# Scaling C's fifth and sixth tile, and one more scan's lam-multiples, on ScalarE in place of VectorE

## The chip, the core and the metric

The kernel runs on one core of a Trainium2 chip. A core has a matrix engine (TensorE, PE in the profile, with its weight loads as PEld), a vector engine (VectorE, DVE), a scalar engine (ScalarE, ACT), a general engine (GpSimd, POOL) and a queue engine (SyncE, SP). POOL and SP issue most of the DMA transfers here. Each engine takes its instructions in the order in which they are written; between engines, semaphores tell when a result, a buffer or a transfer is ready. The metric is the device time of one launch in microseconds (us), the median over runs.

## The reference

Two sequence models run on the same input x (2048 steps, 1024 channels, bf16), and a gate mixes them.

```python
x = A_x
g = sigmoid((x * gate_w).sum(-1, keepdims=True))

# a: a diagonal state space model with 1024 complex states
dt = exp(log_dt);  Lam_bar = exp(dt * Lam);  B_bar = ((Lam_bar - 1) / Lam)[:, None] * Bmat
Bu = einsum("bld,pd->blp", x, B_bar)
h_t = Lam_bar * h_{t-1} + Bu_t                      # for all 2048 steps
a = 2 * einsum("blp,dp->bld", h, Cmat).real + x * Dskip

# b: a short convolution of k (4 taps), times v, then a long convolution by FFT
kv = shift_conv(k, shift_k) * v
b = x * (irfft(rfft(kv) * rfft(ssm_k))[:2048] + kv * ssm_D)

out = g * a + (1 - g) * b
```

## The kernel before, in words

The first 200 us or so compute the long convolution b, by matrix products with tables of cosines, channel block by channel block, and store it in device memory (`cv_scr`). The change lies in what follows: the state space model.

**Tiles.** Time is cut into four blocks of 512 steps, each split into even and odd steps (256 each). The 1024 states are cut into four groups (g = 0 to 3) of two tiles of 128 states. C is therefore eight tiles, `CT[0]` to `CT[7]`, each with a real and an imaginary half of 128 x 1024; group g of the states uses tiles 2g and 2g + 1. B's factor and the factor 2 are folded into C: `turn_C(pi)` (line 1274) multiplies tile pi by a complex number per state. It writes the cross terms (C times `mc2i`) to two buffers `m` on ScalarE, scales C's halves in place by `c2r` and `mc2r`, and adds the two, for tiles 0, 1, 4 and 5 by a DMA that accumulates (`gather`, line 126, issued by POOL; the traces show it as `CT<-Q`), for the others by an addition on VectorE. For tiles 4 and 5, "C's fifth and sixth tile", the `m` buffers come from the pool `Q` of four buffers (line 1337); the traces name them `Q`.

**A Bu unit.** For one time block and one state tile, 16 matrix products fill a bank group of the accumulators (`both`, four such groups rotate), and ScalarE evicts it in two parts to the even steps V and the odd steps O of a tile U. `Bu_next` (line 1365) issues two units per pair of time block and group, and after each unit up to two "fillers": pieces of work taken from the list `on_act` (line 1443).

**A turn.** `turn_U` (line 872) adds lam times the odd steps before to the even steps, so that a scan over even steps alone suffices. It does so in two parts; each writes a buffer of the pool `Q` on ScalarE and adds it to V by a DMA (`U<-Q`). The second part's DMA writes what the first one wrote, and so waits for its landing.

**A scan.** `scan(tb, g, fin)` (line 891) is all VectorE: two products with cosines and sines, two sums, four scan instructions (`W`), and the way back to `hb`, the states at even steps. The states at odd steps are lam times `hb` plus O: four multiplies by lam into two buffers q (`scaled`, line 947), and three additions into O (`summed`, line 956). The list `scaled_by_act` (line 889) names the scans whose multiplies ScalarE does: scan 4 (counted over time block and group, 16 in all) and scans 12, 13 and 14. For these, `scaled` is called later from the main loop, and `summed` in the next scan, behind its four scan instructions (line 922). The buffers q come from VectorE's work pool, but for scans 12 to 14 from the pool `Q`.

**C times the states.** The product with C runs over rows of 128 steps in `psy`: the first two rows of a time block read `hb`, the last two read the odd steps. For the first time block it goes row by row (units C0 to C3), for the second and third group by group (units G10 to G23, where G23 is the third block's group 3), and the last block is done at the end. ScalarE evicts each row of a block times the gate (`scale_a`), and only then can its accumulator banks be used again. The row's part of b is loaded (`loads`: `pbb`, `xr`), scaled on ScalarE (`scale_b`), multiplied by x on VectorE (`product`) and added by a DMA.

**The order.** It is written out by hand. A loop over the 16 scans (j) advances scan j, runs the two tiles of C that are due, issues a turn, and then the units of `plan[j]` (line 1383): j = 1 has the Bu units B9 and B10, j = 2 has B11, j = 3 has B12, B13 and C0; j = 11 has G20, j = 12 has G21 to G23. The turns are set by `turned` (line 1385): turn 14 belongs to j = 10, turn 15 to j = 11. A pool gives its buffers in turn, in the order in which the program's instructions first use them, and an instruction that is to write a buffer waits until its last reader, here often a DMA, is through.

Of the kernel before, what the change touches and what calls it, by code (L numbers as in the profile page):

```python
# [20 lines left out]
def kernel(  # L21
# [39 lines left out]
    NTB = S // TB  # L61
# [30 lines left out]
    def put(eng, f, *a, **kw):  # L92
        with tc.issue_after(prev[eng]) if eng in prev else nullcontext():
            i = f(*a, **kw)  # L94
        prev[eng] = getattr(i, "ins", i)
# [4 lines left out]
    def bc(ap, shape):  # L100
        return ap.to_broadcast(shape)
# [3 lines left out]
    def tt(o, a, b, op):  # L105
        put("dve", V.tensor_tensor, out=o, in0=a, in1=b, op=op)
# [7 lines left out]
    def copy(o, a):  # L114
        put("dve", V.tensor_copy, o, a)

    def act(o, i, **kw):
        put("act", nc.scalar.activation, out=o, in_=i, **kw)
# [7 lines left out]
    def gather(o, i):  # L126
        put("pool", nc.gpsimd.dma_start, out=o, in_=i, accum_op=ALU.add)
# [628 lines left out]
    def carry(tb):  # L756
        q1 = consts.tile([128, 2, NP], F32, name="q1", tag="q1")
        q2 = consts.tile([128, 2, NP], F32, name="q2", tag="q2")
        w = WL[tb - 1]
        tt(q1, w, bc(cs["cU"][:, None, :], [128, 2, NP]), ALU.mult)  # L760
        tt(q2, w, bc(cs["sU"][:, None, :], [128, 2, NP]), ALU.mult)
        tt(init[tb][:, 0], q1[:, 0], q2[:, 1], ALU.subtract)
        tt(init[tb][:, 1], q1[:, 1], q2[:, 0], ALU.add)
# [122 lines left out]
            yield  # L886

    put_off = []
    scaled_by_act = (4, 12, 13, 14)

    def scan(tb, g, fin):


        last = tb == NTB - 1 and g == NG - 1
        Ve, Uo = Us[tb, g]
        A = w2([128, 2, 2, HB], BF16, "A")
        W = None

        for js in ([slice(0, 1), slice(1, 2)] if last else [slice(0, 2)]):
            g2 = slice(2 * g + js.start, 2 * g + js.stop)  # L900
            full = [128, 2, js.stop - js.start, HB]
            Aj, Uj = A[:, :, js], Ve[:, :, js]
            tt(Aj, bc(TC[:, g2][:, None], full), Uj, ALU.mult)
            if js.start == 0:
                yield
            b = w2([128, 2, 2, HB], BF16, "trn")[:, :, js]
            tt(b, bc(TS[:, g2][:, None], full), Uj, ALU.mult)
            if js.start == 0:
                if g == 0 and tb > 0:
                    carry(tb)  # L910
                step(fin)
            tt(Aj[:, 0], Aj[:, 0], b[:, 1], ALU.add)
            tt(Aj[:, 1], Aj[:, 1], b[:, 0], ALU.subtract)
            if W is None:
                W = w2([128, 2, 2, HB], BF16, "W")
            for j in range(js.start, js.stop):
                pi = 2 * g + j
                for c in range(2):
                    put("dve", V.tensor_tensor_scan, out=W[:, c, j], data0=bc(rv2[:, pi:pi + 1], [128, HB]),
                        data1=A[:, c, j], initial=0.0 if tb == 0 else init[tb][:, c, pi:pi + 1],  # L920
                        op0=ALU.mult, op1=ALU.add)
            while put_off:
                put_off.pop()[1]()
            if js.start == 0:
                run(fin)
                hbs[tb, g] = s5p["hb"].tile([128, 2, 2, HB], BF16, name="hb")
            hb = hbs[tb, g][:, :, js]
            Wj = W[:, :, js]
            tt(hb, bc(TC[:, g2][:, None], full), Wj, ALU.mult)
            if tb < NTB - 1:  # L930
                copy(WL[tb][:, :, g2], Wj[:, :, :, HB - 1])
            b = w2([128, 2, 2, HB], BF16, "trn")[:, :, js]
            tt(b, bc(TS[:, g2][:, None], full), Wj, ALU.mult)
            if not last:
                yield
            tt(hb[:, 0], hb[:, 0], b[:, 1], ALU.subtract)
            tt(hb[:, 1], hb[:, 1], b[:, 0], ALU.add)
            by_act = tb * NG + g in scaled_by_act
            if tb * NG + g == 3:
                run(turning[7])  # L940
                product(0)
            if by_act and tb == NTB - 1:
                q = [s5p["Q"].tile([128, 2, 2, HB], BF16, name="Q") for k in range(2)]
            else:
                q = [w2([128, 2, 2, HB], BF16, "q") for k in range(2)]

            def scaled(q=q):
                for k in range(2):
                    for j in range(js.start, js.stop):
                        a = (q[k][:, :, j], hbs[tb, g][:, :, j], lam[:, k, 2 * g + j:2 * g + j + 1])  # L950
                        if by_act:
                            act(a[0], a[1], func=ACT.Identity, scale=a[2])
                        else:
                            ts(*a, None, ALU.mult)

            def summed(q=q, js=js):
                o, (q1, q2) = Uo[:, :, js], [x[:, :, js] for x in q]
                tt(o, o, q1, ALU.add)
                tt(o[:, 0], o[:, 0], q2[:, 1], ALU.subtract)
                tt(o[:, 1], o[:, 1], q2[:, 0], ALU.add)  # L960

            if by_act:
                put_off.append((scaled, summed))
            else:
                scaled()
                summed()
# [66 lines left out]
    def product(t_):  # L1033
        pbb, xr = ios[t_]
        tt(xr, xr, pbb, ALU.mult)
# [4 lines left out]
    def store(t_):  # L1040
        move(rows_of(of, t_), gas.pop(t_))
# [23 lines left out]
    def step(gen):  # L1065
        next(gen, None)

    def run(gen):
        for _ in gen:
            pass  # L1070
# [203 lines left out]
    def turn_C(pi):  # L1274
        by_sum = pi in (0, 1, 4, 5)
        if pi in (4, 5):
            m = [s5p["Q"].tile([128, D], BF16, name="Q") for c in range(2)]
        else:
            whole_m = m_pool.tile([128, 2, D], BF16, name="m")
            m = [whole_m[:, c] for c in range(2)]  # L1280
        for c in range(2):
            act(m[c], CT[pi][:, 1 - c], func=ACT.Identity, scale=mc2i[:, pi:pi + 1])
            yield
        for c, f in enumerate((c2r, mc2r)):
            if pi < 2:
                act(CT[pi][:, c], CT[pi][:, c], func=ACT.Identity, scale=f[:, pi:pi + 1])
            else:
                ts(CT[pi][:, c], CT[pi][:, c], f[:, pi:pi + 1], None, ALU.mult)
            if by_sum:
                gather(CT[pi][:, c], m[c])  # L1290
        if not by_sum:
            tt(CT[pi], CT[pi], whole_m, ALU.add)

    turning = [turn_C(pi) for pi in range(NP)]
    load_BT(3, 0)
    load_BT(3, 1)
# [45 lines left out]
    def w2(shape, dt, name):  # L1342
        return wk.tile(shape, dt, name=name, tag="w2")
# [11 lines left out]
    on_act = []  # L1355
# [77 lines left out]
    for j in range(NS):  # L1433
        for k in loaded.get(j, ()):
            loads(k)
        if j == 7:
            store(3)
        for k in stored.get(j, ()):
            store(k)
        advance(j)  # L1440
        for t in turning[2 * j:2 * j + 2]:
            run(t)
        on_act += [lambda t=t: step(t) for t in turning[2 * j + 2:2 * j + 4] for _ in range(2)]
        turn = turns_U[turned[j]] if j in turned else none
        if j != 10 and plan[j][0:1] != "G":
            step(turn)
        by_group = plan[j][0:1] == "G" and j != 10
        if j == 7:
            scale_b(6)
        if by_group:  # L1450
            for n, k in enumerate(scaled_b.get(j, ())):
                if n == 1:
                    step(turn)
                scale_b(k)
            run(turn)
        if j == 4:
            put_off[-1][0]()
            scale_b(3)
        for unit in plan[j].split():
            if unit == "C0":  # L1460
                scale_b(2)
            if unit[0] == "G":
                Cy_group(int(unit[1]), int(unit[2]))
            else:
                (Bu_next if unit[0] == "B" else Cy_row)(int(unit[1:]))
        if put_off and j not in (4, 12):
            put_off[-1][0]()
        if j == 10:
            step(turn)
            for k in scaled_b[j]:  # L1470
                scale_b(k)
            run(turn)
        elif not by_group:
            run(turn)
            if j == 5:
                run(turns_U[5])
            for k in scaled_b.get(j, ()):
                scale_b(k)
        if j == 7:
            gate(3)  # L1480

    tb = NTB - 1
# [46 lines left out]
```

## Time and profile before

| | |
|---|---|
| median of 3 runs | 384.33 us (384.24 to 385.03) |
| the profiled execution, its own time | 384.57 us |
| its span, first to last instruction | 382.8 us |
| TensorE busy | 371.3 us (97%) |
| VectorE busy | 371.2 us (97%) |
| ScalarE busy | 303.6 us (79%) |
| GpSimd busy | 81.8 us (21%) |

The page gives busy times, the span in 40 slices, the chain of work that ended last, and groups of instructions. In a line such as `CT<-CT,c2r 128x1024 bf16` the tile written stands before the arrow, those read behind it. All operations go through a few helpers on one line of the kernel (L94), so groups are told apart by their tiles. Times in a timeline are counted from the span's start; a row "x4" merges four instructions, its length running from the first start to the last end, and consecutive instructions of VectorE and ScalarE overlap a little, so that the step from one start to the next is shorter than one instruction's length. A bracket at the end of a row gives the idle time of the engine before it and what ended that.

Where things stand in the timeline: the Bu units of j = 1 to 3 run on TensorE from 217.4 to 252, C0 begins at 253.2, G22 at 337.0, G23 at 343.9, the last time block at 350.8, and the last matrix product ends at 378.6.

### The profile page before, as it was taken

How to read it: one execution, taken by the hardware profiler on the slowest of the kernel's cores; microseconds unless marked ns; L12 is line 12 of the kernel's file. 1: busy time of each engine (PE TensorE's matmuls, PEld its weight loads, DVE VectorE, ACT ScalarE, POOL GpSimd, SP SyncE). 2: the span in 40 equal slices, each digit the busy share in tenths (PEclk: the TensorE clock that was granted, in tenths of full speed). 3: DMA queues.
4: the chain of work that ended last, by engine and by line, in shares of the span. 5: the costliest groups of instructions: out<-in, count | busy, mean ns of one | idle time of the engine just before them, and what ended most of it. 6: DMA issues, size and time to landing. Idle time of an engine off the chain costs nothing.

```text
span 382.8 us, 6633 instructions
## 1 busy us (share of the span) xinstructions
PE 371.3 (97%) x2419; PEld 198.3 (52%) x2453; DVE 371.2 (97%) x599; ACT 303.6 (79%) x469; POOL 81.8 (21%) x108
## 2 busy tenths in 40 slices
PE   7899999999999999999999999989999999999995
PEld 5566458575584846744454444434444444444442
DVE  7999999999999999999999999999999999999996
ACT  5898998988979999786979699675989759937601
POOL 4011030020301102031003110413414323634100
PEclk9999999999999999999999999999999999999999
DMA  7979999998999997959999999986899999898903
GB/s 166 165 108 223 218 205 205 245 203 211 201 164 211 208 213 169 198 125 154 192 221 164 226 203 250 213 153 125 150 222 192 208 245 246 136 250 156 238 8 110
DMA packets 126402, 71.77 MB, mean 187 GB/s; under 512 B 104665, under 2 KB 107489, under 8 KB 126370
## 3 DMA queue, kind: packets, MB, share of 16 engines
q1 hardware_dynamic: 111232, 45.64, 55.4%
q0 software_dynamic: 12976, 25.17, 38.9%
q10 hardware_dynamic: 2162, 0.54, 0.8%
q8 instruction: 19, 0.31, 0.3%
q14 instruction: 13, 0.11, 0.1%
HBM read 15.48 MB, written 8.39 MB: 62 GB/s over the span
## 4 chain that ended last, share of the span: by engine, by line
PE 52%; DVE 30%; issue 9%; DMA 4%; ACT 3%; ACTq 1%; POOL 0%; DVEq 0%; POOLq 0%
PE psy L94 29%; PE both L94 15%; DVE BT L94 11%; DVE wkh L94 8%; DVE G L94 5%; DVE t L94 3%; PE psz L94 2%; DVE ks L94 2%; PE psk L94 2%; DMA CT<-Q 2%; DMA pbb<-cv_scr 1%; PE psv L94 1%; DMA rows<-in_gate_w_dram 1%; PE p L94 1%; PE taps L94 1%
## 5 line engine op out<-in xcount | busy, mean ns | idle before, releaser
L94 PEld LDWEIGHTS <-BT 128*128 128x128 bf16 x640 | 62.0, 98 | 48.3 <-issue 0.2
L94 PE MATMUL both<-xT,BT 128*128 128x512 bf16 x375 | 83.0, 379 | 0.4
L94 POOL DMA_DIRECT2D U<-Q x26 | 26.7, 1039 | 88.8 <-ACT Q L94 31.0
L94 PEld LDWEIGHTS <-hb 128*128 128x128 bf16 x256 | 24.9, 98 | 31.4 <-issue 1.6
L94 PEld LDWEIGHTS <-U 128*128 128x128 bf16 x240 | 23.5, 98 | 28.3
L94 PE MATMUL psy<-CT,hb 128*128 128x512 bf16 x157 | 36.3, 379 | 0.1
L94 ACT ACTIVATE Vh<-psv 128x1024 bf16<-128x1024 f32 x32 | 30.7, 1034 | 5.3 <-PE psv L94 5.3
L94 PE MATMUL psy<-CT,U 128*128 128x512 bf16 x149 | 34.6, 379 | 0.2
L94 ACT ACTIVATE Q<-U,lam 128x512 bf16<-128x512 bf16 (+1 forms) x52 | 29.9, 612 | 4.9 <-DMA CT<-Q 4.9
L94 DVE TENSOR_TENSOR_SCAN W<-rv,init,A 128x256 bf16<-128x256 f32 x48 | 32.2, 730 | 0.0
L94 POOL DMA_DIRECT2D G<-wkh x8 | 9.7, 1218 | 102.8 <-DVE wkh L94 102.8
L94 ACT ACTIVATE U<-both 128x512 bf16<-128x512 f32 x44 | 24.1, 595 | 8.0 <-PE both L94 7.5
L94 PEld LDWEIGHTS <-SF 128*128 128x128 bf16 x184 | 18.0, 98 | 19.7 <-issue 1.4
L94 PE MATMUL psk<-eok,SF 128*128 128x512 bf16 (+1 forms) x119 | 27.9, 354 | 0.3
L94 PE MATMUL psz<-G,CI 128*128 128x512 bf16 x64 | 24.3, 379 | 0.1
L94 PE MATMUL psz<-G,SI 128*128 128x512 bf16 x64 | 24.3, 379 | 0.0
L94 PE MATMUL psy<-CTa,hb 128*128 128x512 bf16 x94 | 22.6, 379 | 1.2 <-ACT U L94 1.0
L94 PE MATMUL taps<-dg,kT 128*128 128x128 bf16 (+1 forms) x352 | 21.7, 210 | 0.8 <-DMA kT<-in_B_k_dram 0.8
L94 PEld LDWEIGHTS <-kT 128*128 128x128 bf16 x352 | 21.0, 100 | 2.5 <-DMA kT<-in_B_k_dram 2.1
L94 DVE TENSOR_TENSOR wkh<-BT,Vh 128x3072 bf16<-128x3072 bf16 (+4 forms) x20 | 21.8, 1110 | 0.0
L94 DVE TENSOR_TENSOR wkh<-Kh,Vh 128x3072 bf16<-128x3072 bf16 (+2 forms) x16 | 21.2, 1348 | 0.0
L94 PE MATMUL psy<-CTa,U 128*128 128x512 bf16 x87 | 20.4, 379 | 0.1
(227 smaller groups left out, 846.1 us busy)
## 6 DMA issues: line engine op xcount, KB each, us to landing
U<-Q POOLq DMA_DIRECT2D x26, 256.0 KB, 5.3
G<-wkh POOLq DMA_DIRECT2D x6, 768.0 KB, 8.8
cv_scr<-cv SPq DMA_DIRECT2D x16, 256.0 KB, 5.7
kn<-in_B_ssm_k_dram SPq DMA_DIRECT2D x5, 512.0 KB, 4.0
v<-in_B_v_dram SPq DMA_DIRECT2D x5, 512.0 KB, 6.2
out_dram<-m SPq DMA_DIRECT2D x8, 256.0 KB, 4.5
BT<-cv_scr SPq DMA_DIRECT2D x7, 256.0 KB, 5.9
out_dram<-BT SPq DMA_DIRECT2D x7, 256.0 KB, 2.0
```

What stands on the lines that cost most here:

```text
L94: i = f(*a, **kw)
```

## The change

Three edits belong together. First, `scaled_by_act` gets scan 11, the third time block's group 3: its four multiplies by lam are done by ScalarE, called at the end of the loop's pass j = 11, and its three additions move into scan 12. Its buffers q now come from the pool `Q` (the condition `tb > 1` in place of the last time block alone). Second, in `turn_C` the scaling by `c2r` and `mc2r` goes to ScalarE for tiles 0, 1, 4 and 5 (it was there already for 0 and 1), and a `yield` behind each half's `gather` cuts this work into pieces that can be fillers. Third, the fillers: tiles 4 and 5 are listed at j = 1 with four pieces each in place of two, so that scaling and additions go out between the Bu units of j = 1 and 2; at j = 0 nothing is listed any more (there tiles 2 and 3 were listed, whose pieces had run by the time the first filler was called).

```diff
-    scaled_by_act = (4, 12, 13, 14)
+    scaled_by_act = (4, 11, 12, 13, 14)
...
-            if by_act and tb == NTB - 1:
+            if by_act and tb > 1:
                 q = [s5p["Q"].tile([128, 2, 2, HB], BF16, name="Q") for k in range(2)]
             else:
                 q = [w2([128, 2, 2, HB], BF16, "q") for k in range(2)]
...
         for c, f in enumerate((c2r, mc2r)):
-            if pi < 2:
+            if by_sum:
                 act(CT[pi][:, c], CT[pi][:, c], func=ACT.Identity, scale=f[:, pi:pi + 1])
             else:
                 ts(CT[pi][:, c], CT[pi][:, c], f[:, pi:pi + 1], None, ALU.mult)
             if by_sum:
                 gather(CT[pi][:, c], m[c])
+                yield
...
-        on_act += [lambda t=t: step(t) for t in turning[2 * j + 2:2 * j + 4] for _ in range(2)]
+        if j > 0:
+            on_act += [lambda t=t: step(t) for t in turning[2 * j + 2:2 * j + 4] for _ in range(4 if j == 1 else 2)]
```

## The prediction

> **What bounds the kernel now.** I read the page first (shares of engines), then busy time by stretches, the waits, the chain of work that ended last, and then the timelines of single engines where the change lies.
>
> ```profile
> PE 371.3 (97%) x2419; PEld 198.3 (52%) x2453; DVE 371.2 (97%) x599; ACT 303.6 (79%) x469; POOL 81.8 (21%) x108
> 240.00:248.00 8.00, 8.00 (x39) 3.63 (x37) 7.89 (x20) 5.59 (x8) 3.26 (x5) 1.00 0.92 213
> 248.00:256.00 8.00, 6.91 (x33) 3.07 (x32) 7.93 (x16) 5.43 (x13) 2.11 (x3) 1.00 1.10 205
> 336.00:344.00 8.00, 7.95 (x38) 3.63 (x37) 7.93 (x19) 2.44 (x3) 3.46 (x4) 1.00 1.05 260
> ```
>
> The three lower lines are stretches: length, then busy time of TensorE, its weight loads, VectorE, ScalarE and POOL, the granted clock, the DMA share and GB/s. TensorE and VectorE are both full: 7.8 to 8 of 8 us in every stretch, but for TensorE at 248 to 256. ScalarE has room. Two full engines mean that work taken from one gains nothing by itself, and that any stall of either is felt.
>
> ```profile
> ACT Q L94 <- DMA CT<-Q: 4.9, 1, 4.9
> PE psy L94 <- ACT U L94: 1.0, 1, 1.0
> ...
> 244.74 5.78 DMA CT<-Q
> ...
> 251.17 0.71 ACT Q L94
> ...
> 253.15 9.01 PE psy L94 x41
> ...
> 374.96 3.63 PE psy L94 x16
> 378.62 0.75 DVE BT L94
> ```
>
> The first two lines are waits (us, times, longest), the rest the chain by start and length. At 244.74 the additions into C's fifth and sixth tile go out (they waited for VectorE's scaling), land at 250.5, ScalarE waits 4.9 us for the buffers that they read, evicts late, and TensorE starts `psy` late. From 253.15 to 378.6 TensorE runs without a gap and sets the end.
>
> ```profile
> 329.88 2.52 POOL L94 DMA_DIRECT2D U<-Q  x1
> 340.54 0.86 POOL L94 DMA_DIRECT2D U<-Q  x1 [7.25 <-DMA U<-Q]
> U<-Q POOLq DMA_DIRECT2D x1, 256.0 KB, 10.1
> U<-Q POOLq DMA_DIRECT2D x1, 256.0 KB, 6.0
> 345.63 2.56 ACT L94 ACTIVATE Q<-hb,lam 128x512 bf16<-128x512 bf16 x4 [7.19 <-DVE hb L94]
> 334.41 1.14 DVE L94 TENSOR_SCALAR q<-hb,lam 128x512 bf16<-128x512 bf16 x4
> 335.47 1.48 DVE L94 TENSOR_TENSOR U<-U,q 128x1024 bf16<-128x1024 bf16 x3
> 342.40 0.66 DVE L94 TENSOR_TENSOR row<-row 128x1024 bf16<-128x1024 bf16 x1
> 347.34 3.62 PE L94 MATMUL psy<-CT,U 128*128 128x512 bf16 x16
> 378.62 1.41 DVE L94 SCALAR_TENSOR_TENSOR BT<-psy,gcols,xlast 128x512 bf16<-128x512 f32 x2 [0.42 <-PE psy L94]
> ```
>
> The third and fourth line give the time from issue to landing of the two gathers above them, so turn 14's gathers land at 339.98 and 346.54. The ScalarE line is scan 12's multiples; the VectorE lines are scan 11's multiples and sum, and the first operation behind scan 12's scans. The last line: VectorE idles only 0.42 us before its last work.
>
> **Part 1, C's fifth and sixth tile.** (That j = 0 lists no fillers any more removes calls that did nothing: tiles 2 and 3 were through before the first filler ran.) VectorE loses four multiplies, 243.96 to 245.55: 1.59 us. ScalarE gets four of the kind of `m<-CT`, two of which take 2.08 from start to the next start: 4.16. They now stand between the evictions of the four `both` units of j = 1 and 2, each tile's pair behind the second of its units. ScalarE was busy from 225.51 to 245.53 with 0.14 idle; with 4.16 more, less that 0.14, it is through at 249.5. The first loads it needs earlier are there: the imaginary half of the fifth tile is issued at 220.51 and lands after 5.9, at 226.4; it is wanted at 226.7 (before: 229.16). The gathers go out between 231 and 239, land well before 249, and the wait of 4.9 us is gone: `Q<-U` starts at 249.4, not 250.54. TensorE follows its eviction as before: 253.15 - 1.12 = 252.03. Its units run from 217.41, 160 matmuls at 0.2157, to 251.9, so 0.1 of the wait stays. No earlier unit is starved: the tightest, the ninth, starts at 245.0 and needs an eviction that ends near 242.1. On POOL the four gathers pass `pbb<-gd`, which leaves at 241 in place of 237.3; VectorE multiplies that row at 255.9, so nothing waits. On the DMA engines the four gathers (1.3 us each, by the spacing of their landings) now fall among SP's loads of 231 to 243, whose share is already 1.07 there. The tightest of those, row 1's `pbb`, is issued at 235.9, lands after some 6.7 (its median) and with 4 us more at 246.6, and ScalarE wants it at 247.4. If it is later still, TensorE loses up to 1.1 again; the end does not depend on that, as part 2 shows. Part 1 alone: TensorE 1.1 us earlier, VectorE 1.6.
>
> The swap is dear by itself: a multiply of 128x1024 steps on by 0.40 us on VectorE and by 1.04 on ScalarE. [...]
>
> **Part 2, scan 11's multiples.** VectorE loses four multiplies (334.41 to 335.47, 1.06). Its sum (three additions, 1.39) moves behind scan 12's four scans. ScalarE gets four multiplies, 2.47 (the row of scan 12, start to next start), in its queue behind turn 15 and ahead of row 14's scaling, scan 12's multiples and the evictions of the third time block.
>
> What decides is where the multiples are written. They no longer go to the work pool but to the `Q` pool, four buffers. The changed program's instructions show which they get: those of turn 14, and the first pair waits for the landing of turn 14's first gather, the second pair for its second. In the old kernel scan 12 had these two buffers and found the second free at 346.54, just before it wrote it (346.87). Scan 11 wants it some 9 us earlier. So:
>
> - VectorE reaches the sum at 342.40 - 1.59 - 1.06 - 1.39 = 338.4.
> - The gathers move with their cause. Each second gather of a turn waits for the first one's landing, and so back to ScalarE at 266.68, which waits for scan 4's `hb` on VectorE, 1.6 earlier. I take the shift as 1.6: landings at 338.4 and 344.9.
> - ScalarE writes the first pair at 338.4 to 339.8 (VectorE waits 1.4), the second at 344.9 to 346.3 (VectorE waits 5.9, with one addition between). The last two additions take 0.7: VectorE does `row<-row` at 347.0 in place of 342.40, 4.6 late.
> - All that VectorE has left is in the old order and without a gap, so it ends 4.6 late less the 0.42 it idled: **4.2 us later**.
> - TensorE: the `U` that it wanted at 347.34 - 1.1 = 346.2 comes at 346.8. Then scan 12's `hb` ends at 345.54 + 4.6 = 350.2, its multiples on ScalarE 350.2 to 352.7, and only behind these come the evictions, the first done at 353.8. The last block's first matmul needs that bank: 353.9 in place of 350.79, 3.1 late; the second half of scan 15's `hb` adds 0.4. 3.5 is under 4.2: VectorE sets the end.
>
> **Sum.** Against the profiled execution (384.57, span 382.8): 384.57 + 4.2 = 388.8. It stands 0.24 above the median of the runs, 384.33; the forecast is 388.5.
>
> **Bounds.** Unknown are the shift and the landing time of turn 14's second gather. Shift 0: VectorE 6.2 late, end +5.8, 390.1. The shortest landing of any gather from `Q` is 3.3 (the tile's view: 3.3/5.4/10.1): issued at 338.9 it lands at 342.2, VectorE 1.9 late, +1.5, 385.8. I take 6.0, the row of this very gather, since the queue ahead of it is unchanged.
>
> **The rivals.**
> - Faster: the buffers are free in time and TensorE keeps its 1.1 us: 383.2. For it: VectorE is given 2.65 us and ScalarE idles from 338.4 to 345.6. It decides at a second landing of 340.7; the gather would have to land 1.8 us after its issue at 338.9, where none from `Q` took under 3.3. 0.07.
> - No change within measurement: a landing near 340.7 to 341.5. 0.03.
> - The gathers do not move with VectorE: 390.1. For it, the DMA queues are full at 304 to 320 and could hold the pace. Against it, the loads there wait on the same gathers. 0.13.
> - The gathers are quicker once the rest has thinned out: 385.8 to 387. 0.12.
> - TensorE's clock falls. After the last matmul (378.6) the granted clock is 1.00 until 380.8 and 0.50 from 381.0. The new gap before the last block, 350.3 to 353.9, is longer than those 2.4 us. [...] 0.25.
>
> **How the numbers follow.** The forecast itself 0.40, the others as given. 0.2% is 0.77 us, about what a measurement of this kernel can tell from no change: slower by more 0.90, within 0.03, faster 0.07. The range, from the shortest landing to no shift: 385.8 to 390.3.
>
> **What would show it.** ScalarE's `Q<-hb` of scan 11 in two halves near 338.4 and 344.9, with waits of about 3.3 and 5.3 us ended by the DMA `U<-Q`; VectorE waiting some 6 us in one piece at `U<-U,Q` for ScalarE; TensorE with a gap of about 3.5 us before the last block, and none of 1.0 at 252; the last chain on VectorE. The forecast is wrong if turn 14's second gather lands before 341, or if VectorE shows no wait over 1 us.

## The result and the profile after

| | before | after |
|---|---|---|
| median of the runs | 384.73 us (6 runs) | 388.75 us (6 runs) |
| ratio, 95% interval | | 1.0108 [1.0085, 1.0131] |
| the profiled execution, its own time | 384.57 us | 388.58 us |
| its span | 382.8 us | 386.8 us |

The changed kernel is 1.1% slower. The profiled executions differ by 4.01 us, and the last operation of VectorE ends 3.97 us later (384.00 against 380.03), so nearly all of it lies ahead of that operation. Here and below medians are over all runs, while ratios leave out the slow ones, those over 1.5% above the fastest of the same kernel, which is why a high median can stand beside a ratio of 1.

The engines' busy times, from the page of the changed kernel (busy time, share of the span, instructions):

```profile
PE 372.8 (96%) x2419; PEld 198.2 (51%) x2453; DVE 368.8 (95%) x591; ACT 310.5 (80%) x477; POOL 81.6 (21%) x108
```

VectorE lost 2.4 us of work and ScalarE got 6.9 more. TensorE has the same 2419 instructions; the 1.5 us by which it is busy longer are a stretch at a slower clock, shown below. The change did what its diff says; the time came from waiting and from that stretch. Stretches of the changed kernel show where (columns as in the prediction: busy time of TensorE, weight loads, VectorE, ScalarE, POOL, then the granted clock, the DMA share and GB/s):

```profile
240.00:248.00 8.00, 8.00 (x39) 3.64 (x38) 7.89 (x18) 7.94 (x13) 1.09 (x2) 1.00 1.12 235
248.00:256.00 8.00, 7.95 (x38) 3.56 (x38) 7.93 (x17) 7.97 (x15) 1.71 (x2) 1.00 0.80 175
336.00:344.00 8.00, 7.95 (x38) 3.63 (x38) 3.43 (x6) 1.33 (x2) 3.51 (x4) 1.00 1.09 251
344.00:352.00 8.00, 6.13 (x29) 2.67 (x28) 6.30 (x13) 5.83 (x8) 1.74 (x2) 1.00 0.73 129
352.00:360.00 8.00, 6.75 (x24) 2.79 (x25) 7.86 (x16) 6.70 (x10) 3.42 (x4) 0.79 0.69 133
```

At 240 to 256, where part 1 lies, ScalarE is now full and TensorE too: 7.95 of 8 us in place of 6.91. At 336 to 344 VectorE is busy for 3.43 us (before: 7.93) and ScalarE for 1.33: both wait. TensorE loses its time after that, first by standing still, then, in the last stretch, at a lower clock.

The waits of the changed kernel (us, times, longest) from the answers for ScalarE, VectorE and TensorE:

```profile
ACT Q L94 <- DMA U<-Q: 7.4, 2, 5.9
...
DVE U L94 <- ACT Q L94: 6.2, 1, 6.2
...
PE psy L94 <- ACT BT L94: 3.1, 1, 3.1
```

The two waits shown of before, `ACT Q <- DMA CT<-Q` and `PE psy <- ACT U`, are gone, and these three have come. They are one story, as the timelines of ScalarE, VectorE and TensorE tell:

```profile
337.06 1.33 ACT L94 ACTIVATE Q<-hb,lam 128x512 bf16<-128x512 bf16 x2 [1.52 <-DMA U<-Q]
344.30 1.33 ACT L94 ACTIVATE Q<-hb,lam 128x512 bf16<-128x512 bf16 x2 [5.90 <-DMA U<-Q]
349.59 2.56 ACT L94 ACTIVATE Q<-hb,lam 128x512 bf16<-128x512 bf16 x4 [1.88 <-DVE hb L94]
...
338.76 0.67 DVE L94 TENSOR_TENSOR U<-U,Q 128x1024 bf16<-128x1024 bf16 x1
345.67 0.76 DVE L94 TENSOR_TENSOR U<-U,Q 128x512 bf16<-128x512 bf16 x2 [6.24 <-ACT Q L94]
346.34 0.68 DVE L94 TENSOR_TENSOR row<-row 128x1024 bf16<-128x1024 bf16 x1
...
346.52 3.62 PE L94 MATMUL psy<-CT,U 128*128 128x512 bf16 x16
353.19 5.18 PE L94 MATMUL psy<-CTa,hb 128*128 128x512 bf16 x15 [3.06 <-ACT BT L94]
...
382.59 1.41 DVE L94 SCALAR_TENSOR_TENSOR BT<-psy,gcols,xlast 128x512 bf16<-128x512 f32 x2 [0.42 <-PE psy L94]
```

Scan 11's first pair of multiples waits until turn 14's first gather is through, the second pair until its second gather is. VectorE has done one of the three additions by then and stands for 6.24 us; `row<-row` starts at 346.34 in place of 342.40, 3.94 late. Scan 12 is late by that, its multiples stand on ScalarE ahead of the third block's evictions, and TensorE stands for 3.06 us in front of the last block. VectorE's last operation again waits 0.42 us for TensorE, so TensorE sets the end. The chain of work that ended last (start, length, what) runs back through all of it, to the two gathers:

```profile
327.41 9.55 DMA U<-Q
...
337.51 6.70 DMA U<-Q
...
344.30 1.34 ACT Q L94 x2
...
346.43 0.60 DVE row L94
...
352.14 1.01 ACT BT L94
...
353.19 4.10 PE psy L94 x11
...
378.93 3.63 PE psy L94 x16
```

### The profile page after: what moved, and what is told of

Same layout as the page of the kernel before. It is cut to its first block, busy times and chain, and to the rows that moved or that the text cites. A ratio compares the mean times of both kernels' runs of the same rounds, so it can differ in the third digit from the quotient of the medians.

```text
span 386.8 us, 6631 instructions
## 1 busy us (share of the span) xinstructions
PE 372.8 (96%) x2419; PEld 198.2 (51%) x2453; DVE 368.8 (95%) x591; ACT 310.5 (80%) x477; POOL 81.6 (21%) x108
## 4 chain that ended last, share of the span: by engine, by line
PE 42%; DVE 31%; DMA 10%; issue 8%; ACT 6%; POOL 1%; ACTq 1%; DVEq 0%; POOLq 0%
PE both L94 20%; PE psy L94 15%; DVE BT L94 11%; DVE wkh L94 8%; DMA U<-Q 7%; DVE G L94 5%; DVE t L94 2%; PE psz L94 2%; DMA V<-Q 2%; DVE ks L94 2%; PE psk L94 2%; ACT Q L94 2%; DMA rows<-in_gate_w_dram 1%; PE psv L94 1%; PE taps L94 1%
## 5 line engine op out<-in xcount | busy, mean ns | idle before, releaser
L94 PE MATMUL psy<-CTa,hb 128*128 128x512 bf16 x94 | 24.1, 399 | 3.2 <-ACT BT L94 3.1
L94 ACT ACTIVATE Q<-hb,lam 128x512 bf16<-128x512 bf16 x16 | 10.3, 711 | 13.7 <-DMA U<-Q 7.4
```

## The experiments

Each ratio is against runs of the kernel before on the same chip.

| kernel | median, us | ratio [95%] |
|---|---|---|
| part 1 alone | 384.49 | 0.9990 [0.9962, 1.0018] |
| part 1's places, VectorE scales | 384.30 | 0.9977 [0.9943, 1.0012] |
| part 2 alone | 389.56 | 1.0128 [1.0103, 1.0152] |
| part 2 alone, work pool | 385.57 | 1.0012 [0.9985, 1.0038] |
| the change, work pool | 386.78 | 0.9998 [0.9959, 1.0037] |
| the same, again | 385.17 | 0.9996 [0.9974, 1.0017] |
| the change, only the second pair in the work pool | 385.19 | 0.9997 [0.9971, 1.0023] |
| the change, TensorE's gap filled | 388.82 | 1.0099 [1.0069, 1.0129] |
| before, one spare buffer | 383.89 | 0.9968 [0.9939, 0.9996] |
| the same, again | 383.70 | 0.9964 [0.9944, 0.9985] |

### Part 1 alone

```diff
 # the changed kernel, with two of its lines as before
-    scaled_by_act = (4, 11, 12, 13, 14)
+    scaled_by_act = (4, 12, 13, 14)
...
-            if by_act and tb > 1:
+            if by_act and tb == NTB - 1:
```

> Part 1 alone: C's fifth and sixth tile as in the changed kernel, scan 11 as before. If the whole loss is scan 11's wait for turn 14's buffers: no wait of ScalarE for the DMA CT<-Q, TensorE's gap of 1.0 at C0 gone, 1.1 us faster than before (ratio 0.997). If moving the multiplies to the slower engine costs by itself: as slow as before or slower (1.000 to 1.005). If the earlier additions hold up other transfers: ScalarE late at j = 3, and the gap at C0 as before (1.000).

No change that can be measured; the interval, 0.9962 to 1.0018, still holds the 0.997 that was expected. In its trace VectorE is well ahead: `row<-row` starts at 340.31, 2.09 earlier than before. It gets nothing for it, as the last pieces of the chain show:

```profile
196.35 6.29 DMA BT<-in_A_B_im_dram
202.68 12.26 PE both L94 x56
214.94 3.45 PE psz L94 x16
218.40 34.53 PE both L94 x160
252.93 27.69 PE psy L94 x128
280.62 13.81 PE both L94 x64
295.22 83.07 PE psy L94 x384
```

TensorE runs from 202.68 to the end without a wait. C0 does not wait for ScalarE any more. This execution ends only 0.30 us earlier on TensorE than before's, since TensorE waited 1.18 us for a load of B at 202, which before's profiled execution did not. What that wait hides can be read by counting from the first `psz` matmul behind it: C0 starts 39.19 us after it in before's execution (253.15 less 213.96), 38.06 us after it here (252.84 less 214.78) and as much in the changed kernel (252.33 less 214.27). So TensorE does get the 1.1 us that were forecast for part 1.

### Part 1's places, with VectorE scaling

```diff
 # against part 1 alone
-            if by_sum:
+            if pi < 2:
                 act(CT[pi][:, c], CT[pi][:, c], func=ACT.Identity, scale=f[:, pi:pi + 1])
```

> Part 1's place without its engine: the fifth and sixth tile are scaled between the Bu units of j = 1 and 2 as in the changed kernel, but by VectorE; scan 11 as before. If it is the early release of the Q buffers that pays: the same as part 1 alone, 1.1 us faster than before (0.997), ScalarE through earlier by 4. If it is VectorE's 1.6 us: no faster than before (1.000).

Again no change that can be measured: the interval, 0.9943 to 1.0012, holds both values that were expected, 0.997 and 1.000. ScalarE's row for the turn, from the timeline, has no wait and starts 4.0 us earlier than before's (250.54); TensorE starts C0 behind the Bu units without one:

```profile
246.54 1.32 ACT L94 ACTIVATE Q<-U,lam 128x512 bf16<-128x512 bf16 x2
...
248.69 4.26 PE L94 MATMUL both<-xT,BT 128*128 128x512 bf16 x19
252.79 2.75 PE L94 MATMUL psy<-CTa,hb 128*128 128x512 bf16 x12
```

So the wait of 4.9 us went because the additions go out earlier, not because ScalarE does the scaling.

### Part 2 alone

```diff
 # against the kernel before
-    scaled_by_act = (4, 12, 13, 14)
+    scaled_by_act = (4, 11, 12, 13, 14)
...
-            if by_act and tb == NTB - 1:
+            if by_act and tb > 1:
```

> Part 2 alone: scan 11 by ScalarE with its multiples in Q, C's tiles scaled as before. If the wait for turn 14's second landing sets the loss: that landing is later than in the changed kernel, which got 1.6 us from part 1, so VectorE is 5 to 6 late and the kernel 5 to 6 us slower than before (1.013 to 1.016). If the two parts only add by engine load: slower by less than the changed kernel (under 1.010).

All of the loss is here, at the lower edge of what was expected (1.0128, expected 1.013 to 1.016); the rival's less than 1.010 lies outside the interval. The timelines of ScalarE and VectorE:

```profile
338.77 1.33 ACT L94 ACTIVATE Q<-hb,lam 128x512 bf16<-128x512 bf16 x2 [2.67 <-DMA U<-Q]
345.18 1.33 ACT L94 ACTIVATE Q<-hb,lam 128x512 bf16<-128x512 bf16 x2 [5.08 <-DMA U<-Q]
...
346.55 0.76 DVE L94 TENSOR_TENSOR U<-U,Q 128x512 bf16<-128x512 bf16 x2 [5.72 <-ACT Q L94]
347.23 0.69 DVE L94 TENSOR_TENSOR row<-row 128x1024 bf16<-128x1024 bf16 x1
```

Turn 14's second gather lands at 345.10 here and at 344.21 in the changed kernel; `row<-row` follows 2.13 us behind in both, so it is 0.89 later here and not the 1.6 that part 1 was thought to be worth. TensorE stands 3.42 us before the last block, its granted clock is 1.00 on average over 344 to 352 and 0.79 over 352 to 360, and its last matmul ends 4.97 us later than before's. With part 1 the median is 0.8 us lower (388.75 against 389.56), but the two were not run side by side and the intervals of the two ratios overlap, so what part 1 is worth here isn't settled.

### Part 2 alone, and the whole change, with the work pool

```diff
 # against part 2 alone, and in a second kernel against the changed one
-            if by_act and tb > 1:
+            if by_act and tb == NTB - 1:
```

> Part 2 alone, with the multiples in the work pool: VectorE is given 1.06 us, nothing waits. If TensorE's unbroken run from C0 sets the end, this is worth nothing: as before within 0.2% (1.000). If VectorE is the bound at the end: 1 us faster (0.997).

> The changed kernel with one edit undone: scan 11's multiples are written to VectorE's work pool again and not to Q; ScalarE still does them. If the wait for turn 14's buffers is the whole loss: ScalarE's waits of 1.5 and 5.9 and VectorE's of 6.2 gone, last block without a gap, TensorE bounds throughout, 1.1 us faster than before (0.997), so 5 us faster than the changed kernel. If ScalarE's load (2.5 us more, ahead of the evictions) makes the loss: still 2 to 4 us slower than before (1.005 to 1.010).

ScalarE and VectorE do the same work in the same order; only the buffers of scan 11's multiples come from the work pool. From the timelines of part 2 with the work pool:

```profile
338.38 2.55 ACT L94 ACTIVATE q<-hb,lam 128x512 bf16<-128x512 bf16 x4
...
340.58 1.53 DVE L94 TENSOR_TENSOR U<-U,q 128x1024 bf16<-128x1024 bf16 x3
342.30 0.69 DVE L94 TENSOR_TENSOR row<-row 128x1024 bf16<-128x1024 bf16 x1 [0.18 <-DMA row<-gd]
```

The multiples run through, no wait for a gather is left, and the loss is gone in both kernels: 1.0012 and 0.9998. It wasn't the slower multiply on ScalarE, nor its place in the queue. For part 2 with the work pool that is what was expected if TensorE bounds the kernel. The 0.997 expected of the whole change did not show: 0.9998, and 0.9996 when it was run again, where the interval begins at 0.9974.

The whole change with the work pool had times far apart, from 383.26 us up. Its profiled execution took 390.76 us, which says nothing of the median; in it the load of the fifth tile's imaginary half came late, ScalarE waited 3.0 us for it ahead of the evictions, and C0 came late. To see whether that is what parts the times, it was run again:

> The same kernel as the change with the work pool, once more, since its times lay far apart (383.3 to 387.7, and some higher). Theory: the times part by the loads of C. If the imaginary half of the fifth tile lands before 227, ScalarE waits under 0.7 us for it, C0 has no gap over 0.3 us, the granted clock is 1.00 from 8 to 380 us, and the time is 383.3 to 385. If it lands after 229, ScalarE waits over 2 us ahead of evictions, TensorE has a gap of 2 to 3 us at C0, and the time is over 386. Rival (the scatter comes from elsewhere): an execution over 386 without that wait, or one under 385 with it.

As the whole cause that theory fell, though the execution of 390.76 us fits it. This profiled execution took 386.50 us, and ScalarE's multiply of the fifth tile has no wait. TensorE was late before the change begins:

```profile
198.77 1.46 PE L94 MATMUL both<-xT,BT 128*128 128x512 bf16 x6
201.92 1.90 PE L94 MATMUL both<-xT,BT 128*128 128x512 bf16 x8 [1.70 <-DMA BT<-in_A_B_re_dram]
204.25 2.12 PE L94 MATMUL both<-xT,BT 128*128 128x512 bf16 x9 [0.43 <-DMA BT<-in_A_B_im_dram]
```

It waits for B, as part 1 alone did, as part 2 with the work pool did (1.66 and 0.66 us at 202 to 205), and as the kernel before with a spare buffer did in its first profile (1.21 us), which has neither part of the change. Against the execution of 383.34 us of the next experiment, the first `psz` matmul starts 2.51 us later (216.35 against 213.84) and the last matmul of all 3.15 later (380.11 against 376.96); a gap of 0.56 at C0 is most of the rest. Nothing behind the late loads of B made up for them here. That explains this execution; of the others there is no trace.

### Which of the two gathers

```diff
 # against the changed kernel
-                q = [s5p["Q"].tile([128, 2, 2, HB], BF16, name="Q") for k in range(2)]
+                q = [s5p["Q"].tile([128, 2, 2, HB], BF16, name="Q") for k in range(2 if tb == NTB - 1 else 1)]
+                if tb < NTB - 1:
+                    q.append(w2([128, 2, 2, HB], BF16, "q"))
```

> The change, with scan 11's first pair of multiples in a buffer of the pool Q (turn 14's first) and its second pair in the work pool. Theory (the whole price is the landing of turn 14's second gather, at 344 to 345): ScalarE waits for the first gather, to about 337 to 338.7, and writes the second pair at once; VectorE waits 1.5 us at most at U<-U,Q, does row<-row by 341, TensorE has no gap over 0.6 us before the last block, clock 1.00; 383.3 to 386.5 us, as with all four in the work pool. Rival (any use of pool Q for scan 11 costs, since scan 12 is moved on by a buffer): scan 12's second pair gets turn 15's first buffer, whose gather lands at 347 to 349, and waits up to 2 us; the evictions of the third block come late, TensorE has a gap of 1 to 2.6 us before the last block; 386 to 388.

Scan 11's first pair still waits for turn 14's first gather, its second pair has a buffer that is free. ScalarE and VectorE, from the timelines:

```profile
336.69 1.33 ACT L94 ACTIVATE Q<-hb,lam 128x512 bf16<-128x512 bf16 x2 [1.57 <-DMA U<-Q]
337.93 1.32 ACT L94 ACTIVATE q<-hb,lam 128x512 bf16<-128x512 bf16 x2
343.93 1.33 ACT L94 ACTIVATE Q<-hb,lam 128x512 bf16<-128x512 bf16 x2 [2.60 <-DMA U<-Q]
346.44 1.33 ACT L94 ACTIVATE Q<-hb,lam 128x512 bf16<-128x512 bf16 x2 [1.18 <-DMA U<-Q]
...
339.28 0.76 DVE L94 TENSOR_TENSOR U<-U,q 128x512 bf16<-128x512 bf16 x2 [0.52 <-ACT q L94]
339.96 0.69 DVE L94 TENSOR_TENSOR row<-row 128x1024 bf16<-128x1024 bf16 x1
```

One buffer takes the whole loss away: VectorE waits 0.52 us, `row<-row` is 2.44 earlier than before, TensorE has no gap before the last block, and the ratio is 0.9997. The rival was right on ScalarE, where scan 12's two pairs now wait 2.60 and 1.18 us, but not on the time: its additions wait 0.12 us for them. So the price was the landing of turn 14's second gather: in the changed kernel VectorE is ready for the second pair at 339.43, the gather lands 4.78 us later, and the pair takes ScalarE another 1.46.

In this execution B came in time, as in before's profiled one, so the two can be compared from end to end. The first line is before's, the others are this kernel's; before's C0, at 253.15, stands in the prediction:

```profile
213.96 0.38 PE L94 MATMUL psz<-G,CI 128*128 128x512 bf16 x1
...
213.84 0.38 PE L94 MATMUL psz<-G,CI 128*128 128x512 bf16 x1
...
251.91 2.75 PE L94 MATMUL psy<-CTa,hb 128*128 128x512 bf16 x12
```

C0 starts 1.24 us earlier than before's, 0.12 of which is there at `psz` already, and the last matmul ends 1.24 us earlier too (377.34 against 378.58), as does VectorE's last operation. So in these traces the 1.1 us forecast for part 1 reach the end once the buffer is free. The ratio doesn't show it: 0.997, its size, is the very end of the interval.

### The clock

```diff
 # against the changed kernel: behind the third block's last row, 14 matmuls with a tile of zeros
+    still = consts.tile([128, 128], BF16, name="still")
+    nc.gpsimd.memset(still, 0.0)
...
-            Cy_g(tb, tl, [ps[:, 0], ps[:, 1]], g, g == NG - 1)
+            warm = tb == 2 and tl == 3 and g == NG - 1
+            Cy_g(tb, tl, [ps[:, 0], ps[:, 1]], g, g == NG - 1 and not warm)
+            for n in range(14 if warm else 0):
+                mm(ps[:, n % 2], still, CT[7][:, 0, 0:512], False, n >= 12)
```

> The changed kernel with 14 products of a zero tile added behind the third block's last row (0.216 us each, 3.0 in all; they add nothing to the sums), in TensorE's gap of 3.2 us before the last block. If the fall of the clock to 0.50 set the end: the clock stays at 1.00, TensorE is 1.6 earlier, VectorE's 3.9 late less its idle 0.42 takes over: 0.4 to 0.5 us faster than the changed kernel, with no wait of VectorE before its last operation. If VectorE set the end anyway: the same time as the changed kernel. If the clock goes by more than activity of this kind: it falls as before.

TensorE doesn't idle before the last block, as the stretch of the last block's start has it:

```profile
352.00:360.00 8.00, 7.95 (x38) 3.63 (x38) 7.86 (x16) 6.70 (x10) 3.42 (x4) 1.00 0.67 129
```

And VectorE's timeline:

```profile
346.42 0.69 DVE L94 TENSOR_TENSOR row<-row 128x1024 bf16<-128x1024 bf16 x1
...
380.94 2.60 DVE L94 SCALAR_TENSOR_TENSOR BT<-psy,gcols,xlast 128x1024 bf16<-128x1024 f32 x3
```

In this stretch the granted clock stays at 1.00 (changed kernel: 0.79), the last matmul ends 1.13 us earlier (381.43 against 382.55), and VectorE's last operation no longer waits. The profiled execution is 0.49 us shorter (388.09), and that is all: VectorE, 4.02 late at `row<-row`, now sets the end 3.51 us later than before. In the medians nothing of it shows (388.82 against 388.75). Between these two executions the fall of the clock is worth half a microsecond; the wait alone costs 3.5.

### A spare buffer in the kernel before

The same kind of wait stood in the kernel before, at 250.5, where the turn of j = 3 waits for the buffers that C's additions read. Here its first part writes to a buffer of another pool:

```diff
 # turn_U, against the kernel before
-                Q = s5p["Q"].tile([128, 2, 2, HB], BF16, name="Q")
+                if Us[1, 2][0] is V_ and part[0][0] == both:
+                    Q = s5p["hb"].tile([128, 2, 2, HB], BF16, name="hb")
+                else:
+                    Q = s5p["Q"].tile([128, 2, 2, HB], BF16, name="Q")
```

> The kernel before, with one buffer changed: the first half of the turn of j = 3 (turn 8) is written to a spare buffer of the pool of hb in place of Q, so that ScalarE need not wait for the DMA CT<-Q. If that wait alone made TensorE's gap at C0: gap gone, 1.2 us faster than before (0.997), with all multiplies where they were. If VectorE's lateness or the load of ScalarE made it: unchanged (1.000).

> The kernel before with one buffer of turn 8 taken from the pool hb, once more: it had been the fastest so far. Theory (TensorE sets the end of the kernel before, and without its wait of 1.0 us before C0 the end comes about 1 us sooner): 383.6 to 384.2, ratio 0.996 to 0.998 with the interval below 1. Rival (VectorE ends at the same time as TensorE, within 0.4 us, so no more than that is to be had): ratio 0.999 to 1.000.

It beats the kernel before by 0.3 to 0.4%, twice with the interval below 1, as both theories said. In the first profile ScalarE's wait is gone too, but B was late by 1.21 us, so C0 starts at 253.16 and the end comes where before's does. In the second profile ScalarE writes that buffer at 245.58 without a wait, TensorE starts C0 at 252.00 (before: 253.15), and at the end VectorE doesn't wait for TensorE:

```profile
376.52 2.59 DVE L94 SCALAR_TENSOR_TENSOR BT<-psy,gcols,xlast 128x1024 bf16<-128x1024 f32 x3
```

Of the 0.91 us by which VectorE ends earlier here than in before's profile, 0.35 is there at `row<-row` already, and 0.42 is the wait that is gone. So VectorE sets the end here, as the rival had it, and the wait that is gone is as long as the rival's bound. But the gain is larger than that bound: the medians differ by 1.1 us, and 0.999 lies outside the interval of the second round. What the rest is isn't settled.

## Why the prediction was right, point by point

- **Slower, 388.5 (385.8 to 390.3).** Measured 388.75. The mechanism forecast, a wait for the buffers of turn 14 that takes the place of VectorE's four multiplies, is the one that the traces and the two kernels with another pool show.
- **Part 1.** Both waits went as forecast: `Q<-U` starts at 249.73 without a wait (forecast 249.4), and C0 starts at 252.33 without one (forecast 252.03, with the first `psz` matmul 0.31 later in this execution). TensorE's 1.1 us are there in the traces; that they shorten part 1 alone is neither shown nor excluded by its 0.9990. VectorE's share gained nothing there: it was 2.09 early, and TensorE set the end.
- **The swap of engines.** By the steps that the prediction read, a multiply of 128x1024 takes 1.04 us on ScalarE and 0.40 on VectorE, and both parts together put 6.6 us on ScalarE for the 2.65 that they take from VectorE, 4.0 more. The whole change with the work pool has the same swap and measures 0.9998 and 0.9996: here the swap cost nothing that could be measured. ScalarE had the room (80% busy in the changed kernel).
- **The buffers and the second wait.** ScalarE waits 5.90 us for the second gather (forecast 5.3), VectorE 6.24 in one piece (5.9). Right. For the first gather ScalarE waits 1.52, not 3.3.
- **"I take the shift as 1.6."** Mis-sized, and its reason not borne out. The second gather lands 2.33 earlier than before (344.21 against 346.54), so `row<-row` is 3.94 late and not 4.6. The shift was derived from VectorE's 1.59 us at scan 4. But part 2 alone, where scan 4's multiples start only 0.09 earlier, has 1.44, and the kernel with a spare buffer 1.29 and 1.15; part 1 alone has 4.20. The changed kernel, part 1 alone, the kernel with the filled gap and the one with only the second pair in the work pool issue the same work up to turn 14, and this gather lands at 344.21, 342.34, 344.30 and 343.83. So it moves by up to 2 us from one execution to the next, more than the 0.7 by which the shift was off. No run separates what moves the gathers.
- **"VectorE waits 1.4" for the first pair.** It didn't: the first gather landed at 336.96 and the pair was written before VectorE came at 338.76. It would have cost nothing in any case, since the second landing decides.
- **"VectorE sets the end", 4.2 late.** This step failed. VectorE alone is 3.94 - 0.42 = 3.5 late, as the kernel with the filled gap shows (3.51). TensorE, forecast at 3.5, came 3.97 late: it resumed 2.40 later than before (353.19 against 350.79) and then ran 3.2 us, to 356.41, at half clock, which is 1.6 more. That is the rival that had been given 0.25, and the gap had been priced at 3.1. No trace of before shows how long the clock stays down within the kernel; here it was 3.41 us. The 0.4 forecast for the second half of scan 15's `hb` did not show: TensorE has no wait behind 353.19. The two ends lie within half a microsecond of each other. So the mechanism of the wait was right, but that the sum meets the time so closely is partly luck: VectorE's lateness was 0.7 less than forecast, and the slower clock made up 0.45 of it.
- **The range.** No run here shows the ends: neither a landing without any shift (390.1) nor one after 3.3 us (385.8). Turn 14's second gather took 5.1 to 6.9 us from issue to landing in the twelve profiles, so the 6.0 taken for it holds.

## What to carry to other kernels

Before an operation is moved to another engine, list who last reads the buffers that it will write and when that reader is through: here one of the two pairs of multiplies, put behind a transfer in flight, cost 1.1%, and the same work with another buffer cost nothing. Where two engines end within half a microsecond of each other, as here, 1.06 us of work taken from VectorE alone gained nothing that could be measured (1.0012), and a stall longer than that was paid. In the three executions in which TensorE stood for 2.8 to 3.4 us within the kernel (2.82, 3.06 and 3.42), the granted clock was 0.79 on average over the 8 us in which it went on (352 to 360, for the gap of 2.82 us 256 to 264). In the changed kernel that was 3.41 us at 0.50, which by an estimate from that length costs up to 1.7 us more. The executions with stalls of 1.18, 1.66 and 1.70 us at 200 to 203 have mean granted clocks of 0.998, 1.000 and 0.999 over the whole span (before: 0.998), those three have 0.993 to 0.996.

## What was not expected of the hardware

The moment at which the granted clock fell. In the changed kernel TensorE stopped at 350.13, the clock was 0.50 from 352.99 to 356.41, and TensorE was back at work from 353.19: only 0.2 of the 3.41 us lay in the gap, 3.2 on the last block's first matmuls. In part 2 alone the gap of 3.42 us ended at 354.08, in the change with the work pool that of 2.82 us at 257.64. The mean granted clock was still 1.00 in the 8 us that end within these gaps (344 to 352 and 248 to 256) and 0.79 in the next 8.

Behind the last matmul the clock fell to 0.50 at 380.96 in before's execution, 2.38 us after TensorE's end at 378.58, and at 387.13 in the changed kernel's, 4.58 us after its end at 382.55. Within the changed kernel it was 2.86 us. So in these two executions the clock did not fall one and the same time after TensorE stopped; what sets the moment no run here shows.
